# The third batch's k, q and v asked for behind the last weight tile, in a fused pack attention and softplus layer

## The chip, the core and the metric

The kernel runs on one core of a Trainium2 chip. Its engines are TensorE (PE in the rows; its weight loads are PEld), VectorE (DVE), ScalarE (ACT), GpSimd (POOL) and SyncE (SP), which here only issues DMA transfers. The metric is the device time of one execution in microseconds (us), lower is better.

## The reference

Attention goes through a small set of 32 "pack" queries per head: the packs attend to the sequence, and then each query attends to the packs. A two-layer network with softplus follows.

```python
batch, n_heads, seq, head_dim = (8, 8, 576, 64)
n_pack = 32
def sm_attn(qq, kk, vv):
    s = scale * np.matmul(qq, kk.transpose(0, 1, 3, 2))
    s = s - np.max(s, axis=-1, keepdims=True)
    a = np.exp(s)
    a = a / (np.sum(a, axis=-1, keepdims=True) + 1e-09)
    return np.matmul(a, vv)
p_packed = sm_attn(p, k, v)
out = sm_attn(q, p_packed, p_packed)
...
n_tokens, d_model, d_ff = (4608, 512, 2048)
h = x @ w_in
g = np.maximum(h, 0.0) + np.log1p(np.exp(-np.abs(h)))
return (g @ w_out).astype(np.float32)
```

The weights `w_in` and `w_out` come as float64; the other inputs and the output are float32.

## The kernel before

**Units.** The work is a list of units (b, f): batch b of 8, and f one of 16 blocks of 128 hidden columns. In a unit `gemm1` (L511) multiplies the attention output of the batch by a block of the first weights into two PSUM tiles `ph`, `softplus` (L546) turns them into `e` on ScalarE and VectorE and splits `e` into a high and a low part `gh` and `gl`, and `gemm2_tile` (L569), two units later, adds their products with `w_out` into four accumulators `acc`. There are two `ph` buffers, so a unit's first product waits until the softplus step of the unit before has read them (L558). The four accumulators have one buffer each: a batch's first product into `acc` 2 waits until the last batch's `acc` 2 has been copied out to `o` (L588, in `store`).

**The attention of the next batch** is a generator, `attention(b)`; its steps are drawn between the tiles of the units of batch b - 1. For batches 0 and 1 the transposes of k and q are made on TensorE, from batch 2 (`BY_BLOCK`) on by VectorE (L253), from k and q loaded in four parts of 32 rows each (L133). `load` (L114) is called from within the generator, early: the k and v of batch b + 1 are asked for while batch b's attention runs, so those of batch 2 during the units of batch 0. All these loads share four buffers (`ld`); a load waits for the reader of the buffer's last content.

**The first weights are folded.** `make_m` (L482) multiplies the packed values of a batch by `w_in` itself, and the result takes the place of the first weights. For batch 0 it does so for 256 columns at a time, products 0 to 7 (`psm_0_c`); product c is emitted at the end of unit 2c - 2, and its halves `mh` and `ml` serve units 2c and 2c + 1.

**The weights are converted on the chip** during batch 0 by the generator `convert` (L162), 32 tiles in the order i0 i1 o0 o1 i2 i3 o2 o3 and so on (i of `w_in`, o of `w_out`). A tile is loaded as raw 64-bit words into `x_i` or `x_o` (`load64`, L140; from the ninth on two buffers serve), read twice by ScalarE (L188 makes `m`, L192 makes `r`), put together by VectorE (L194, L199) and GpSimd (L207), which writes `w_in_sb` or `t`. The load of tile n + 2 reuses the buffer of tile n. Product 7 of batch 0 needs tiles i14 and i15, numbers 28 and 29 of the order.

**What sets the order.** TensorE's instructions run in the order in which they are written. On the other engines, SyncE's queue among them, the framework's scheduler sets the order when the kernel is built; each engine then runs its queue strictly in that order.

## Time and profile before

| | us |
|---|---|
| median of 3 runs | 789.79 (789.66 to 790.73) |
| the profiled execution | 791.07 |
| its span, first to last instruction | 789.2 |
| TensorE busy | 744.0 (94%) |
| VectorE busy | 532.9 (68%) |
| ScalarE busy | 436.5 (55%) |

The table is read from the top: how long the kernel takes, how long the one execution took that the profile describes, and how much of its span each engine worked. An engine that is busy nearly all the time bounds the kernel over the whole, but single stretches can have another limit.

### The profile page before, as it was taken

Reading aid. Unit: us, or ns where it says so; the run is one execution under the profiler, and the core shown is the slowest. Engines: PE = TensorE matmul, PEld = TensorE weight load, DVE = VectorE, ACT = ScalarE, POOL = GpSimd, SP = SyncE. Lnnn points to the kernel's source line nnn. Section 1 sums busy time; section 2 is a strip of 40 time slices with the busy share of each in tenths; the row PEclk is TensorE's granted clock in tenths of the full one; section 3 lists DMA queues with packets and bytes.
Section 4 is the critical chain, followed back from the end, with each engine's and each line's share of the span. In section 5 each row is a group of like instructions: output and inputs, shape, how many; then the busy total and the mean of one; then the engine's idle time right before and its main releaser. Section 6 shows DMA issues by size and latency. Waiting matters only on the chain.

```text
span 789.2 us, 14442 instructions
## 1 busy us (share of the span) xinstructions
PE 744.0 (94%) x5436; PEld 589.1 (75%) x5436; DVE 532.9 (68%) x1264; ACT 436.5 (55%) x1085; POOL 91.2 (12%) x166
## 2 busy tenths in 40 slices
PE   6879978399999999999999999999999999999997
PEld 4756756287778877887878787877788777878886
DVE  2688758767578665977487665966597656865554
ACT  5678856466556264566556265565555354555540
POOL 1415322210000000000000000000000000000010
PEclk9799989599999999999999999999999999999999
DMA  9976746703421242124411151124312210010002
GB/s 219 245 178 178 165 110 134 153 14 85 68 53 31 68 74 49 31 48 85 74 31 32 66 90 33 32 71 80 56 31 44 67 17 2 1 54 1 1 1 67
DMA packets 163397, 55.97 MB, mean 71 GB/s; under 512 B 143872, under 2 KB 156672, under 8 KB 163328
## 3 DMA queue, kind: packets, MB, share of 16 engines
q1 hardware_dynamic: 162784, 54.93, 32.3%
q8 instruction: 42, 0.69, 0.4%
q14 instruction: 27, 0.22, 0.1%
q10 hardware_dynamic: 544, 0.13, 0.1%
HBM read 45.61 MB, written 9.44 MB: 70 GB/s over the span
## 4 chain that ended last, share of the span: by engine, by line
PE 75%; DVE 1%; ACT 1%; DMA 0%; issue 0%; ACTq 0%; DVEq 0%
PE acc L571 38%; PE ph L527 23%; PE acc_m L571 6%; PE psm L490 3%; PE ps L270 2%; PE psp L325 1%; PE psa L315 1%; DVE at_l L472 1%; ACT e L554 0%; ACT e L553 0%; DMA out<-o 0%; DVE e L558 0%; ACT e L555 0%; ACT at_h L286 0%; PE psx L338 0%
## 5 line engine op out<-in xcount | busy, mean ns | idle before, releaser
L553 ACT ACTIVATE e<-ph 128x288 f32<-128x288 f32 x256 | 103.0, 402 | 213.5 <-PE ph L527 190.8
L558 DVE SCALAR_TENSOR_TENSOR e<-ph,e 128x288 f32<-128x288 f32 x256 | 113.7, 452 | 153.4 <-ACT e L555 153.1
L571 PE MATMUL acc<-wo_h,gh 128*128 128x512 f32 x512 | 208.1, 407 | 0.4 <-DVE o L588 0.4
L571 PE MATMUL acc<-wo_h,gl 128*128 128x512 f32 x512 | 201.1, 393 | 0.0
L571 PE MATMUL acc<-wo_l,gh 128*128 128x512 f32 x512 | 201.1, 393 | 0.0
L527 PE MATMUL ph<-at_h,mh 128*128 128x288 f32 x512 | 159.0, 311 | 3.9 <-DVE e L558 3.1
L527 PE MATMUL ph<-at_l,mh 128*128 128x288 f32 x512 | 153.6, 300 | 2.5 <-DVE at_l L472 2.4
L527 PE MATMUL ph<-at_h,ml 128*128 128x288 f32 x512 | 152.8, 298 | 0.0
L527 PEld LDWEIGHTS ph<-at_h,mh 128*128 128x128 f32 x512 | 97.6, 191 | 40.9 <-issue 13.6
L571 PEld LDWEIGHTS acc<-wo_h,gh 128*128 128x128 f32 x512 | 96.6, 189 | 26.3 <-issue 9.8
L564 POOL COPY rest<-e 128x64 f32<-128x64 f32 x128 | 46.2, 361 | 587.5 <-DVE e L558 581.5
L571 PEld LDWEIGHTS acc<-wo_h,gl 128*128 128x128 f32 x512 | 96.3, 188 | 21.6
L554 ACT ACTIVATE e<-e 128x288 f32<-128x288 f32 (+1 forms) x240 | 109.2, 455 | 3.5
L555 ACT ACTIVATE e<-e 128x288 f32<-128x288 f32 (+1 forms) x240 | 109.4, 456 | 2.9
L571 PEld LDWEIGHTS acc<-wo_l,gh 128*128 128x128 f32 x512 | 96.7, 189 | 13.1
L527 PEld LDWEIGHTS ph<-at_l,mh 128*128 128x128 f32 x512 | 97.9, 191 | 7.2 <-DVE at_l L472 4.5
L527 PEld LDWEIGHTS ph<-at_h,ml 128*128 128x128 f32 x512 | 97.8, 191 | 0.0
L544 DVE TENSOR_TENSOR gl<-e,gh 128x512 fp32r<-128x512 f32 x128 | 87.0, 680 | 5.3
L490 PE MATMUL psm<-w_in_sb,pt 64*32 64x512 f32 (+1 forms) x576 | 39.4, 569 | 23.5 <-POOL w_in_sb L207 20.6
L543 DVE CAST gh<-e 128x512 fp32r<-128x512 f32 x128 | 56.2, 439 | 5.8
L505 ACT CAST mh<-psm 128x512 fp32r<-128x512 f32 (+1 forms) x72 | 35.7, 542 | 43.8 <-PE psm L490 43.6
L506 DVE TENSOR_TENSOR ml<-psm,mh 128x512 fp32r<-128x512 f32 (+1 forms) x72 | 42.8, 622 | 18.6 <-ACT mh L505 18.6
(77 smaller groups left out, 742.8 us busy)
## 6 DMA issues: line engine op xcount, KB each, us to landing
v<-in_v SPq DMA_DIRECT2D x16, 576.0 KB, 5.0
x_i<-in_moe_w_in SPq DMA_DIRECT2D x32, 256.0 KB, 4.8
x_o<-in_moe_w_out SPq DMA_DIRECT2D x16, 512.0 KB, 3.9
k<-in_k SPq DMA_DIRECT2D x48, 144.0 KB, 3.3
q<-in_q SPq DMA_DIRECT2D x48, 144.0 KB, 3.2
out<-o SPq DMA_DIRECT2D x24, 256.0 KB, 2.0
k<-in_k SPq DMA_DIRECT2D x4, 576.0 KB, 9.8
q<-in_q SPq DMA_DIRECT2D x4, 576.0 KB, 8.6
```

The source lines that it names most:

```text
L490: nc.tensor.matmul(ps[hh * J:(hh + 1) * J, :n], res["pt"][g][o:o + D, hh * J:(hh + 1) * J], w_in_sb[o:o + D, hh, c * n:(c + 1) * n], start ...
L505: nc.scalar.copy(mh[:, cols], ps[:, :n])
L506: nc.vector.tensor_tensor(ml[:, cols], ps[:, :n], mh[:, cols].bitcast(F32), op=ALU.subtract)
L527: nc.tensor.matmul(ph[:, :C], x[:, ms], y[:, g, cs], start=(i == 0), stop=(i == 3 * G - 1),)
L543: nc.vector.tensor_copy(hi, x)
L544: nc.vector.tensor_tensor(lo, x, hi.bitcast(F32), op=ALU.subtract)
L553: nc.scalar.activation(es[c], hv[c], AF.Abs)
L554: nc.scalar.activation(e[:, x], e[:, x], AF.Exp, scale=-1.0)
L555: nc.scalar.activation(e[:, x], e[:, x], AF.Ln, bias=1.0)
L558: nc.vector.scalar_tensor_tensor(es[c], hv[c], 0.0, es[c], op0=ALU.max, op1=ALU.add)
L564: nc.gpsimd.tensor_copy(rest[:, rest_at(b, f), r:r + REST], e[:, NT * P:])
L571: nc.tensor.matmul(acc, x[:, cs], y[:, f, :], start=(first and i == 0), stop=(last and i == 2),)
```

## The change

Loads of k, q and v of batch 2 no longer go out when `load` is called. Until the weights are all asked for they are put on a list, `late`; three steps from the end of the conversion's order, where the last tile has just been asked for, `release` issues what is on the list. Those loads, and any of batch 2 that come later, are tied to the last weight load: `tc.issue_after(last_weight.ins)` makes the scheduler place them behind it on SyncE. It adds an order within that queue, and no semaphore. The loads themselves, their sizes and buffers are the same, and nothing is computed differently. Behind the change a line's number is some 9 to 21 higher.

```diff
--- before.py
+++ after.py
@@ -1,5 +1,5 @@
 import math
-from contextlib import ExitStack
+from contextlib import ExitStack, nullcontext
 
 import concourse.bass as bass
 import concourse.tile as tile
@@ -110,10 +110,19 @@
             nc.scalar.copy(dst[D:], ps[:D])
 
     loaded = {}
+    late = []
 
     def load(nm, b, g):
         if b >= B:
             return
+        if late is not None and b == BY_BLOCK:
+            late.append((nm, b, g))
+            return
+        with tc.issue_after(last_weight.ins) if b == BY_BLOCK else nullcontext():
+            load_now(nm, b, g)
+
+    def load_now(nm, b, g):
+
         src = {"q": q, "k": k, "v": v}[nm][b, g * HG:(g + 1) * HG]
         if b < BY_BLOCK:
             t = ld.tile([NP, HG, SI, D], F32, tag="ld", name=f"{nm}_{b}_{g}")
@@ -135,14 +144,24 @@
                 )
         loaded[nm, b, g] = t
 
+    def release():
+
+        nonlocal late
+        late, todo = None, late
+        for x in todo:
+            load(*x)
+
+    last_weight = None
+
     CN = 512
 
     def load64(srcs, nm, tag="x"):
         pool, bufs = (cv, 2) if tag == "x" else (work, 1)
         x = pool.tile([P, CN], I64, tag=tag, name=f"x_{nm}", bufs=bufs)
         n = P // len(srcs)
+        nonlocal last_weight
         for i, src in enumerate(srcs):
-            nc.sync.dma_start(
+            last_weight = nc.sync.dma_start(
                 x[i * n:(i + 1) * n].rearrange("x (a n) -> x a n", a=src.shape[1]), src
             )
         return x
@@ -219,6 +238,8 @@
                 first(n)
                 if n < 6 or n >= 8:
                     prefetch(n + 4 if n < 6 else n + 2)
+                if n + 3 == len(order):
+                    release()
             yield
             w, i = order[n - 1] if n else ("i", 0)
             t = ts.pop(n - 1)[0].bitcast(F32) if n else None
```

Since the scheduler places the instructions of SyncE, ScalarE, VectorE and GpSimd, the change moves more than the loads. Three places follow, first before and then after. A name's numbers are batch, head group and so on; the last one is a buffer number.

SyncE's queue around the last weight tiles, before (`x_i14` is the load of tile 14 of `w_in`):

```order
L133 DMA k_2_1_1397<-in_k 32x36x32 x3
L145 DMA x_o12_1415<-in_moe_w_out 128x512
L145 DMA x_o13_1489<-in_moe_w_out 128x512
L125 DMA v_2_0_1513<-in_v 96x24x64
L145 DMA x_i14_1503<-in_moe_w_in 64x4x128 x2
L145 DMA x_i15_1561<-in_moe_w_in 64x4x128 x2
L145 DMA x_o14_1602<-in_moe_w_out 128x512
L125 DMA v_2_1_1749<-in_v 96x24x64
L145 DMA x_o15_1674<-in_moe_w_out 128x512
L133 DMA q_2_0_2098<-in_q 32x36x32 x4
L98 DMA p_1_4006<-in_p 32x8x64 x4
```

The same place after:

```order
L164 DMA x_o12_1405<-in_moe_w_out 128x512
L164 DMA x_o13_1479<-in_moe_w_out 128x512
L164 DMA x_i14_1493<-in_moe_w_in 64x4x128 x2
L164 DMA x_i15_1549<-in_moe_w_in 64x4x128 x2
L164 DMA x_o14_1590<-in_moe_w_out 128x512
L164 DMA x_o15_1662<-in_moe_w_out 128x512
L142 DMA k_2_0_1664<-in_k 32x36x32 x4
L142 DMA k_2_1_1669<-in_k 32x36x32 x4
L134 DMA v_2_0_1674<-in_v 96x24x64
L134 DMA v_2_1_1749<-in_v 96x24x64
L614 DMA out_0<-o_0_0_2034 96x512
L614 DMA out_0<-o_0_0_2034 32x512
```

The last parts of k, and v, no longer stand between the weight tiles but behind the last of them; q of batch 2 and the second load of p now stand further down, among the stores `out`.

ScalarE around unit 12's softplus, before (`m_26` and `r_26` are the two reads of tile 26 of the order, which is `x_o12`; `e_0_12` is the softplus of unit 12 of batch 0):

```order
L263 COPY T_q_1_1_3_1729<-psT_q_1_1_3_1725 128x288
L555 ACTIVATE e_0_12_1715<-e_0_12_1715 128x576
L188 ACTIVATE m_26_1497<-x_o12_1415 128x512
L192 ACTIVATE r_26_1499<-x_o12_1415 128x512
L192 ACTIVATE r_27_1557<-x_o13_1489 128x512
L188 ACTIVATE m_27_1555<-x_o13_1489 128x512
L226 CAST wo_h_88<-t_26_1501 128x512
L226 CAST wo_h_88<-t_27_1559 128x512
L361 ACTIVATE a2_1_1_0_1756<-a2_1_1_0_1756 128x288
L361 ACTIVATE a2_1_1_1_1763<-a2_1_1_1_1763 128x288
L188 ACTIVATE m_28_1596<-x_i14_1503 128x512
L192 ACTIVATE r_28_1598<-x_i14_1503 128x512
```

After, one unit earlier in the program:

```order
L211 ACTIVATE r_28_1586<-x_i14_1493 128x512
L247 CAST wo_h_88<-t_27_1547 128x512
L526 CAST mh_0_6_0_1610<-psm_0_6_1_1601 128x256
L574 ACTIVATE e_0_11_1630<-ph_0_11_0_1616 128x288
L574 ACTIVATE e_0_11_1630<-ph_0_11_1_1623 128x288
L575 ACTIVATE e_0_11_1630<-e_0_11_1630 128x576
L576 ACTIVATE e_0_11_1630<-e_0_11_1630 128x576
L284 COPY T_q_1_1_1_1644<-psT_q_1_1_1_1640 128x288
L211 ACTIVATE r_29_1658<-x_i15_1549 128x512
L382 ACTIVATE a2_1_0_1_1515<-a2_1_0_1_1515 128x288
L284 COPY T_q_1_1_2_1684<-psT_q_1_1_2_1680 128x288
L207 ACTIVATE m_29_1656<-x_i15_1549 128x512
```

The reads of `x_i14` and `x_i15` (`m_28`, `r_28`, `m_29`, `r_29`) stood behind the end of unit 12's softplus; now they stand around unit 11's.

VectorE at the start of batch 1, where batch 0's output is copied out of the accumulators, before:

```order
L588 COPY o_0_2_2051<-acc_0_2_805 128x512
L558 SCALAR_TENSOR_TENSOR e_1_2_2082<-ph_1_2_0_2068,e_1_2_2082 128x288
L558 SCALAR_TENSOR_TENSOR e_1_2_2082<-ph_1_2_1_2075,e_1_2_2082 128x288
L253 STREAM_TRANSPOSE T_k_2_1_0_2126<-k_2_1_1397 128x288
L588 COPY o_0_3_2062<-acc_0_3_806 128x512
L295 TENSOR_REDUCE m1_2_0_2122<-a1_2_0_1991 128x1
L543 CAST gh_1_2_2128<-e_1_2_2082 128x512
L297 TENSOR_SCALAR nm1_2_0_2124<-m1_2_0_2122 128x1
L253 STREAM_TRANSPOSE T_k_2_1_1_2181<-k_2_1_1397 128x288
L544 TENSOR_TENSOR gl_1_2_2129<-e_1_2_2082,gh_1_2_2128 128x512
L253 STREAM_TRANSPOSE T_k_2_1_2_2193<-k_2_1_1397 128x288
L307 TENSOR_SCALAR rs_2_0_2190<-z1_2_0_2179 128x1
```

After:

```order
L274 STREAM_TRANSPOSE T_k_2_1_0_2126<-k_2_1_1669 128x288
L316 TENSOR_REDUCE m1_2_0_2122<-a1_2_0_1991 128x1
L564 CAST gh_1_2_2128<-e_1_2_2082 128x512
L318 TENSOR_SCALAR nm1_2_0_2124<-m1_2_0_2122 128x1
L274 STREAM_TRANSPOSE T_k_2_1_1_2181<-k_2_1_1669 128x288
L565 TENSOR_TENSOR gl_1_2_2129<-e_1_2_2082,gh_1_2_2128 128x512
L274 STREAM_TRANSPOSE T_k_2_1_2_2193<-k_2_1_1669 128x288
L328 TENSOR_SCALAR rs_2_0_2190<-z1_2_0_2179 128x1
L274 STREAM_TRANSPOSE T_k_2_1_3_2228<-k_2_1_1669 128x288
L329 RECIPROCAL rs_2_0_2190<-rs_2_0_2190 128x1
L609 COPY o_0_2_2051<-acc_0_2_805 128x512
L609 COPY o_0_3_2062<-acc_0_3_806 128x512
```

The copies `o_0_2` and `o_0_3`, which stood ahead of unit 2's softplus step and behind its first k transpose, now stand together behind four k transposes and a reciprocal.

## Rows read from the trace of the kernel before

**Rows 1.** The execution as a whole: span and mean granted TensorE clock.

```profile
core 0: 789.2 us, clock 0.975
```

**Rows 2.** Waits of TensorE in the whole execution: us in total, times, longest.

```profile
PE psm L490 <- POOL w_in_sb L207: 20.6, 3, 15.5
```

**Rows 3.** Stretches: us, busy time by engine (instructions), PEclk, DMA share, GB/s.

```profile
54.50:93.99 39.49, 34.57 (x274) 25.71 (x275) 31.27 (x68) 33.21 (x73) 17.14 (x17) 0.96 0.64 166
93.99:163.26 69.27, 48.37 (x363) 37.48 (x363) 49.23 (x111) 40.92 (x84) 19.43 (x21) 0.83 0.59 129
...
106.25:109.90 3.65, 0.00 (x1) 0.00 (x1) 1.81 (x4) 2.74 (x5) 1.27 (x1) 0.81 0.29 59
109.90:115.26 5.36, 5.36 (x31) 4.27 (x32) 2.40 (x6) 2.61 (x7) 1.27 (x1) 0.50 0.54 159
...
136.27:151.79 15.52, 0.00 (x0) 0.00 (x0) 13.51 (x31) 6.38 (x11) 5.37 (x4) 0.60 0.70 157
151.79:156.30 4.51, 4.51 (x29) 3.61 (x30) 2.37 (x5) 1.76 (x5) 1.27 (x1) 0.50 0.99 189
```

**Rows 4.** Timeline of TensorE: the three products that waited for w_in_sb.

```profile
109.90 1.11 PE L490 MATMUL psm<-w_in_sb,pt 64*32 64x256 f32 x16 [3.65 <-POOL w_in_sb L207]
...
124.98 0.67 PE L490 MATMUL psm<-w_in_sb,pt 64*32 64x256 f32 x16 [1.42 <-POOL w_in_sb L207]
...
151.79 1.11 PE L490 MATMUL psm<-w_in_sb,pt 64*32 64x256 f32 x16 [15.52 <-POOL w_in_sb L207]
```

**Rows 5.** Timeline of SyncE's queue, 117 to 139 us.

```profile
117.09 3.29 SPq L133 DMA_DIRECT2D k<-in_k  x3
120.48 2.45 SPq L145 DMA_DIRECT2D x_o<-in_moe_w_out  x2
122.99 0.42 SPq L125 DMA_DIRECT2D v<-in_v  x1
135.56 3.10 SPq L145 DMA_DIRECT2D x_i<-in_moe_w_in  x4
```

**Rows 6.** Timeline of ScalarE, 134 to 149 us.

```profile
134.30 0.67 ACT L188 ACTIVATE m<-x_o 128x512 f32<-128x512 f32 x1
134.87 1.22 ACT L192 ACTIVATE r<-x_o 128x512 int32<-128x512 uint32 x2
...
148.54 0.65 ACT L192 ACTIVATE r<-x_i 128x512 int32<-128x512 uint32 x1
```

**Rows 7.** DMA issues, 88 to 124 us: count, KB each, median us to landing.

```profile
x_i<-in_moe_w_in SPq DMA_DIRECT2D x8, 256.0 KB, 4.3
x_o<-in_moe_w_out SPq DMA_DIRECT2D x4, 512.0 KB, 3.9
k<-in_k SPq DMA_DIRECT2D x8, 144.0 KB, 4.2
```

**Rows 8.** Timeline of VectorE around the stores of batch 0.

```profile
168.53 0.82 DVE L558 SCALAR_TENSOR_TENSOR e<-ph,e 128x288 f32<-128x288 f32 x2
...
180.47 0.69 DVE L588 COPY o<-acc 128x512 f32<-128x512 f32 x1 [1.42 <-DMA out<-o]
...
182.20 0.65 DVE L588 COPY o<-acc 128x512 f32<-128x512 f32 x1
...
185.21 0.47 DVE L253 STREAM_TRANSPOSE T_k<-k 128x288 f32<-128x288 f32 x1
...
186.77 0.15 DVE L308 RECIPROCAL rs<-rs 128x1 f32<-128x1 f32 x1
```

**Rows 9.** Timeline of TensorE around the same stores.

```profile
169.04 0.40 PE L527 MATMUL ph<-at_h,mh 128*128 128x288 f32 x1
...
181.64 0.40 PE L571 MATMUL acc<-wo_h,gh 128*128 128x512 f32 x1
...
182.91 0.51 PE L571 MATMUL acc<-wo_h,gh 128*128 128x512 f32 x1 [0.41 <-DVE o L588]
```

**Rows 10.** Timeline of ScalarE: the sum of the third batch's first exponential.

```profile
184.69 0.19 ACT L302 ACTIVATION_READ_ACCUMULATOR a<-a,nm 128x1 f32 x1
```

## The prediction

> **What bounds the kernel now.** I read the whole first, then the waits of TensorE, then stretches of time, and then each engine's timeline around the one long wait. The span is 789.2 us at a mean granted clock of 0.975 [rows 1]. TensorE is the bound over the long run, so a wait taken out of it comes off the end, unless another engine fills the hole. The largest wait by far is that of `make_m` for converted columns of `w_in`: 20.6 us in three pieces [rows 2], before products 5, 6 and 7 of batch 0: 3.65, 1.42 and 15.52 us [rows 4]. All three lie in units 7 to 14 of batch 0 (93.99 to 163.26 us), which take 69.27 us while TensorE is busy for 48.37 [rows 3]. The clock adds to it: after the 3.65 and the 15.52 us of idleness TensorE ran 5.36 and 4.51 us at 0.50, the lower of its two levels [rows 3].
>
> Why is tile 15 of `w_in` late? The reader should see that SyncE is not the one that holds it. The queue passes the third batch's k at 117.09 and asks for the `w_out` tiles 12 and 13 from 120.48 on; then it stands still until 135.56 [rows 5]. At that moment ScalarE ends its first read of tile 12: m at 134.30, r from 134.87 (two of 0.61) [rows 6]. There are two staging buffers, so tile 14 of `w_in` can't be asked for before that read. Tiles land in 3.9 to 4.3 us (median) [rows 7], so those asked for from 120.48 lay ready from about 124.5 on, some 10 us before ScalarE came to them. In ScalarE's queue that read stands behind the softplus of unit 12; the order printed above shows it.
>
> **The change, part by part.** Four terms.
>
> (1) *The weights, units 7 to 14.* With the k and v loads out of the way the scheduler sets the reads of the weight tiles earlier: the last `w_in` tile is now read ahead of the softplus of unit 12 and not behind it. So all three waits should go, and with them the slow clock. This is a gain from the order on ScalarE, more than from freed DMA time. Its size lies between bounds. From above: TensorE's own need, 48.37 less at most half of the 9.87 us that it ran at half clock, is 43.4 us, a gain of 25.8. But VectorE is busy for 49.23 us of the same work [rows 3] and can't do it in less; the gain is then 20.0. From below: units 1 to 6, which also convert two tiles a unit and never wait for `w_in`, take 39.49 us, 6.58 each [rows 3]; eight of them are 52.7 us, a gain of 16.6. I take the middle of the last two, 51.3 us, a gain of **18.0**: VectorE has the last softmax and the conversions of all remaining tiles between two softplus steps here, so it becomes the bound, and some of its waits show.
>
> (2) *The third batch's first k on VectorE.* Its four transposes, 0.47 each [rows 8], lay in the 15.52 us hole before, when nobody was delayed. Now the load comes later, and they stand near the end of unit 14, ahead of the low parts of the attention output and of the softplus of unit 15, on which the first product of batch 1 waits: 168.53, with the product at 169.04 [rows 8, 9]. Cover gone: four by 0.47, 1.9 us, less the 0.5 us between that softplus step's start and the product, a loss of about **1.3** (bounds 0, if VectorE has run ahead, and 1.9).
>
> (3) *The copies of the first batch's output.* Before, accumulators 2 and 3 were copied out at 180.47 and 182.20 [rows 8], and TensorE wrote the next accumulators 2 and 3 at 181.64 and 182.91 [rows 9]. Now both copies stand behind four transposes of k and behind a reciprocal that needs the sum of the exponential, which ScalarE gives out at 184.69 plus 0.19 [rows 10]. Counted on the clock of before: that sum is there at 184.9, or some 0.7 earlier, since one copy of 0.65 is out of the way of the maximum that the exponential needs; the transpose behind it and the reciprocal take 0.47 and 0.15 [rows 8]; the copy starts at about 185.1 and ends at 185.8. Accumulator 2 is written from 185.85 in place of 181.64, 4.2 us of a standing TensorE. Accumulator 3 follows 0.7 later, and without its wait of before; at its end the loss is 3.4 us. Nothing hides this: TensorE's queue holds accumulator 2 at its head, and all later work of batch 1 behind it. Loss **3.4**.
>
> (4) *The clock after (3).* The row of 3.65 us of idleness was followed by 5.36 us at 0.50 [rows 3], half of which, at most 2.7, is lost; a standing still of 4.2 us is nearest to that row. I take **2.2**; bounds 0 and 2.7.
>
> Other moves cost nothing that I can find. The second load of p is asked for a batch later, and needed only in batch 3. The third batch's q is asked for around the first stores; its transposes come some units later, behind that batch's second softmax sum, and a load of this kind lands in about 4.2 us [rows 7].
>
> The k, q and v are the same bytes, so nothing else is added. The sum: 18.0 - 1.3 - 3.4 - 2.2 = 11.1 us, a span of 778.1 us. The profiled execution itself took 791.07 us, 1.87 around its span, and lies 1.28 above the median of the three timed runs, 789.79. I take the gain off the median: **778.7 us**.
>
> Is the data now late? At 6.4 us a unit the product 7 falls at about 132.4, and the last tile is asked for about then. Four parts of k at 1.1 us of queue each (three took 3.29 [rows 5]) and 4.2 us to land [rows 7] give 141; the transposes are due near 145.3, the end of unit 14. That leaves some 4 us. The Trainium skill speaks against the change here: its page "DMA: Bandwidth & Descriptors", section "Rules for kernel authors", says to issue a DMA early and to wait for it late, so that its cost lies under compute. By that rule the loads, of which the last k went at 117.09 before and now would go after 132, would show as waits of VectorE, rival D below; the rows leave room for them, so the trace as far as it goes does not bear the rule out here.
>
> **The rivals.**
> A. *TensorE stays the bound.* VectorE's 49.23 us contain the long hole, in which nothing pressed it, so its real need may be smaller. Then (1) gives up to 25.8, and if the clock in (4) also holds, 25.8 - 1.3 - 3.4 = 21.1: 768.7 us. Against it: VectorE was busy for 13.51 of the 15.52 us of that hole [rows 3], so it was not loitering.
> B. *ScalarE stands in front of a tile that has not landed.* The new order puts reads between the parts of the softplus (tile 13 of `w_out` ahead of a logarithm). A tile is asked for when the one two before it has been read, and lands 3.9 to 4.3 us later [rows 7]. If half a landing, 2 us, shows in three of the pairs that are left, 6 us go: 784.7 us. Against it: with two tiles a unit in units 1 to 6 this did not stop the kernel more than the 6.58 us a unit already hold.
> C. *The other side: the wait stays.* If the ring of two buffers holds the tiles back whatever the order, product 7 waits as before and (2) to (4) still cost: 789.8 + 6.9 = 796.7 us. It decides if less than 6.9 of the 25.8 us come back. Against it: the 10 us between landing and read of tile 12 are a matter of order.
> D. *The third batch's k is late* and VectorE stands in front of it with batch 1's weights behind. The change turns slower once this wait is over 11.1 us, that is once the k lands some 15 us later than worked out. If it were 13 us: 791.7 us.
>
> **How the numbers follow.** Chances: my forecast 0.64 (its own range 774.5, with 20.0 in (1) and no clock loss, to 781.2, with 16.6, 1.9 and 2.7), A 0.12, B 0.16, C 0.05, D 0.03. The range leaves out A, C and D: 771 to 785. About 0.2%, 1.6 us, is what a measurement of this kernel can tell from no change. My forecast, A and B are all faster, 0.92; C and most of D are slower, 0.06; a chain of losses that ends within 0.2% has 0.02.
>
> **What would show it.** Right: no wait of `psm` for `w_in_sb` over 2 us; units 7 to 14 in 50 to 53 us; VectorE busy above 0.9 of that stretch; a wait of some 4 us of an accumulator for the copy `o` at the start of batch 1, with a clock of 0.50 behind it. Wrong: a long wait of `psm` for `w_in_sb` still there (C), ScalarE waiting for `x_o` or `x_i` for microseconds (B), VectorE waiting for k (D), or no wait at the copies, by which I would be 5.6 us too high.

## The result, and the profile after

| | before | after |
|---|---|---|
| median of 4 runs, us | 789.72 (789.36 to 790.73) | 779.33 (778.38 to 780.04) |
| ratio after to before | | 0.9866 (95% interval 0.9849 to 0.9883) |
| the profiled execution, us | 791.07 | 778.38 |
| its span, us | 789.2 | 776.6 |

The changed kernel is 10.4 us faster; 11.1 us was forecast, and the time lies 0.6 us above the 778.7 predicted. The mean granted clock is 0.989, and was 0.975 [rows 1].

The stretches of the profile after (us, busy time by engine, granted clock, DMA share, GB/s). The first goes from the start of product 4 of batch 0 to the start of product 0 of batch 1, that is units 7 to 14; the second to product 1 of batch 1:

```profile
92.32:145.41 53.09, 47.55 (x363) 35.61 (x362) 50.95 (x108) 40.66 (x84) 20.96 (x21) 0.97 0.67 152
145.41:169.50 24.09, 20.21 (x129) 15.41 (x128) 18.22 (x43) 12.58 (x32) 1.28 (x5) 0.99 0.16 39
167.65:169.50 1.85, 1.85 (x6) 1.04 (x6) 0.54 (x1) 0.00 (x0) 0.00 (x0) 0.82 0.44 123
169.50:173.48 3.98, 3.98 (x29) 2.31 (x29) 1.29 (x2) 1.58 (x4) 0.00 (x0) 0.65 0.94 186
173.48:190.00 16.52, 16.52 (x148) 13.57 (x147) 9.05 (x22) 9.87 (x28) 0.96 (x3) 1.00 0.26 42
```

Units 7 to 14 take 53.09 us in place of 69.27 [rows 3], and VectorE is busy for 50.95 of them, 96%. Products 5, 6 and 7 in TensorE's timeline (start and duration in us, and in brackets the wait), which answer to [rows 4]:

```profile
104.94 1.19 PE L511 MATMUL psm<-w_in_sb,pt 64*32 64x256 f32 x16
...
117.89 1.29 PE L511 MATMUL psm<-w_in_sb,pt 64*32 64x256 f32 x16 [0.65 <-DVE pt L361]
...
134.68 0.91 PE L511 MATMUL psm<-w_in_sb,pt 64*32 64x256 f32 x16 [0.85 <-DVE a L370]
```

None of the three waits for `w_in_sb` any more; what is left ahead of the last two is 0.65 and 0.85 us for VectorE. SyncE's timeline, to be held against [rows 5]:

```profile
106.97 4.73 SPq L164 DMA_DIRECT2D x_o<-in_moe_w_out  x2
113.14 5.43 SPq L164 DMA_DIRECT2D x_i<-in_moe_w_in  x4
120.41 7.66 SPq L164 DMA_DIRECT2D x_o<-in_moe_w_out  x2
128.12 7.38 SPq L142 DMA_DIRECT2D k<-in_k  x8
```

ScalarE's two reads of tile 12 of `w_out`, against [rows 6]:

```profile
111.88 0.67 ACT L207 ACTIVATE m<-x_o 128x512 f32<-128x512 f32 x1 [0.54 <-ACT r L211]
112.44 0.66 ACT L211 ACTIVATE r<-x_o 128x512 int32<-128x512 uint32 x1
```

Tiles 12 and 13 of `w_out` are asked for at 106.97 and not at 120.48, tile 12 is read from 111.88 and not from 134.30, and the loads of tiles 14 and 15 of `w_in` go out at 113.14 and not at 135.56, again at the moment at which the second read of tile 12 ends. VectorE's timeline up to the stores of batch 0, which answers to [rows 8]:

```profile
147.85 0.47 DVE L274 STREAM_TRANSPOSE T_k<-k 128x288 f32<-128x288 f32 x1
...
150.66 0.82 DVE L579 SCALAR_TENSOR_TENSOR e<-ph,e 128x288 f32<-128x288 f32 x2
...
166.50 0.47 DVE L274 STREAM_TRANSPOSE T_k<-k 128x288 f32<-128x288 f32 x1
166.88 0.12 DVE L329 RECIPROCAL rs<-rs 128x1 f32<-128x1 f32 x1
166.92 1.27 DVE L609 COPY o<-acc 128x512 f32<-128x512 f32 x2
```

TensorE's over the same time, against [rows 9]:

```profile
151.17 0.40 PE L548 MATMUL ph<-at_h,mh 128*128 128x288 f32 x1
...
167.65 0.50 PE L592 MATMUL acc<-wo_h,gh 128*128 128x512 f32 x1 [3.74 <-DVE o L609]
```

The copies of accumulators 2 and 3 stand behind the reciprocal (166.88); accumulator 2 is written at 167.65 after a wait of 3.74 us, and right behind it the clock is at 0.82 and 0.65 for 5.8 us (third and fourth window).

Where the 12.6 us between the two spans come from, by landmarks on TensorE:

| stretch | before | after | gain |
|---|---|---|---|
| start to product 4 of batch 0 | 93.99 | 92.32 | 1.67 |
| units 7 to 14 (product 4 to product 0 of batch 1) | 69.27 | 53.09 | 16.18 |
| product 0 to product 1 of batch 1 | 20.55 | 24.09 | -3.54 |
| from there to the end | 605.4 | 607.1 | -1.7 |

The first line can't be put down to the change: in the executions profiled below, product 4 starts anywhere between 90.1 and 95.6 us, with the program ahead of it the same or nearly so. The comparisons below therefore go by stretches first and by totals second. A stretch is read from the one profiled execution of each kernel, a total from all its runs.

### The profile page after: what moved, and what is told of

It is laid out like the page before. It is cut to its first block, busy times and chain, and to the rows that moved or that the text cites. A ratio compares the mean times of both kernels' runs of the same rounds, so it can differ in the third digit from the quotient of the medians.

```text
span 776.6 us, 14447 instructions
## 1 busy us (share of the span) xinstructions
PE 740.8 (95%) x5436; PEld 584.9 (75%) x5436; DVE 535.9 (69%) x1264; ACT 435.3 (56%) x1085; POOL 92.2 (12%) x166
## 4 chain that ended last, share of the span: by engine, by line
PE 81%; DVE 9%; ACT 4%; DMA 3%; issue 1%; POOL 0%; SPq 0%; ACTq 0%; DVEq 0%; POOLq 0%
PE acc L592 40%; PE ph L548 25%; PE acc_m L592 6%; PE psm L511 4%; PE ps L291 3%; PE psp L346 2%; DMA q<-in_q 1%; PE psa L336 1%; DVE e L579 1%; DVE at_l L493 1%; DVE t L218 1%; ACT e L575 1%; DVE t L213 1%; DMA k<-in_k 1%; ACT e L574 1%
## 5 line engine op out<-in xcount | busy, mean ns | idle before, releaser
L564 DVE CAST gh<-e 128x512 fp32r<-128x512 f32 x128 | 57.8, 452 | 5.5
## 6 DMA issues: line engine op xcount, KB each, us to landing
k<-in_k SPq DMA_DIRECT2D x4, 576.0 KB, 10.4
```

The costliest lines, as they stand in the source:

```text
L564: nc.vector.tensor_copy(hi, x)
```

## Experiments

My theory (T1) was the prediction's: the waits go because ScalarE reads the tiles earlier, VectorE then bounds units 7 to 14, and the copies cost what terms 3 and 4 say. The rivals: what counts is that k is out of the tiles' way (in SyncE's queue or in the DMA engines); VectorE is no bound; the loss at the copies would come back elsewhere. One table for all of them; "units 7 to 14" is the stretch of above, "batch 1" goes from its product 0 to its product 2 (two stretches, for the wait at the copies and the clock behind it), and each total stands beside the kernel before on the same chip. The ratio is an estimate from all runs and need not be the quotient of the two medians.

| kernel | units 7 to 14 | batch 1 | total, median (range) | before there | ratio (95%) |
|---|---|---|---|---|---|
| before | 69.27 | 42.03 | 789.72 | | |
| after | 53.09 | 46.86 | 779.33 | 789.72 | 0.9866 (0.9849 to 0.9883) |
| after, again | 52.89 | 47.62 | 778.98 (777.33 to 782.48) | 792.63 | 0.9838 (0.9799 to 0.9877) |
| reads first | 66.04 | 43.04 | 788.38 (786.25 to 794.84) | 791.85 | 0.9970 (0.9949 to 0.9991) |
| ScalarE's order | 58.01 | 43.02 | 781.92 (779.58 to 785.58) | 790.74 | 0.9893 (0.9867 to 0.9919) |
| copies of bytes | 53.74 | 46.80 | 779.73 (776.88 to 780.51) | 790.56 | 0.9856 (0.9826 to 0.9886) |
| tiny copies | 54.07 | 47.49 | 780.12 (778.74 to 784.05) | 790.56 | 0.9876 (0.9840 to 0.9912) |
| k on GpSimd | 61.98 | 43.23 | 783.93 (783.12 to 786.95) | 792.63 | 0.9901 (0.9872 to 0.9929) |
| no tie | 56.33 | 43.03 | 779.29 (777.35 to 779.77) | 791.85 | 0.9840 (0.9820 to 0.9861) |
| copies o first | 53.44 | 43.48 | 775.74 (775.27 to 775.83) | 791.85 | 0.9799 (0.9780 to 0.9817) |
| without wo_l | 50.13 | 46.85 | 777.65 (776.87 to 779.97) | 792.63 | 0.9819 (0.9793 to 0.9846) |
| wo_l twice | 55.84 | 48.25 | 782.45 (780.39 to 785.31) | 792.63 | 0.9877 (0.9846 to 0.9909) |
| wo_l on GpSimd | 53.97 | 46.84 | 782.62 (778.02 to 788.36) | 791.85 | 0.9892 (0.9858 to 0.9926) |
| gh on ScalarE, copies o first | 52.70 | 45.00 | 775.86 (773.75 to 778.78) | 790.56 | 0.9826 (0.9787 to 0.9865) |

### What ends the wait for the weights

**Reads first.** The kernel before, with one edit in `softplus`:

```diff
-                    nc.scalar.activation(es[c], hv[c], AF.Abs)
+                    n = min(2 * f + 6, 29)
+                    with tc.issue_after(read[n].ins) if b == 0 and 10 <= f <= 12 else nullcontext():
+                        nc.scalar.activation(es[c], hv[c], AF.Abs)
```

(`read[n]` is the second read of tile n.) Expected:

> The kernel before with one thing changed: in units 10 to 12 of batch 0 ScalarE's queue holds the reads of the weight tiles ahead of the softplus of the unit. The loads of the third batch's k and v stay early, between the weight tiles, as before. T1 (the order on ScalarE is what the change gives): the wait of 15.5 us of psm for w_in_sb falls under 2 us, the two waits of 3.7 and 1.4 us may stay, units 7 to 14 take 53 to 58 us in place of 69.3, and the kernel 776 to 781 us. T2 (what counts is that k and v are out of the way of the tiles, in the DMA engines and in SyncE's queue): the long wait stays over 10 us and the kernel takes 787 to 790 us.

Measured: 66.04 us for the stretch, 788.38 us in all. The window of the stretch (columns as above):

```profile
93.24:159.28 66.04, 50.73 (x363) 38.51 (x362) 49.19 (x109) 40.83 (x84) 19.89 (x21) 0.87 0.55 125
```

TensorE's waits in it (us in total, times, longest):

```profile
PE ph L529 <- DVE e L562: 10.2, 4, 7.6
PE psm L492 <- POOL w_in_sb L209: 5.1, 2, 3.7
```

The wait of 15.5 us is gone, as T1 said, but a wait of `ph` for the softplus step, 7.6 us, has come in its place: the softplus of unit 10 now stands behind the reads of tile 12 of `w_out`, which is asked for only at 119.57 (120.48 in the kernel before), so it begins at 126.95, and the products of unit 11 wait for its buffer. My form of T1 falls here. Either this order is a poor one, or the tiles are late for another reason as well.

**ScalarE's order.** The same question with the very order of the changed kernel. A list of 103 names holds ScalarE's instructions of units 5 to 15 in the order that they have there, and each is tied behind the last of those that precede it in the list and are already written:

```diff
+    def act(key, f, *args, **kw):
+        i = place.get(key)
...
+        ahead = [j for j in queued if j < i]
+        with tc.issue_after(queued[max(ahead)]) if ahead else nullcontext():
+            queued[i] = f(*args, **kw).ins
...
-                    nc.scalar.activation(es[c], hv[c], AF.Abs)
+                    act(f"ph_{b}_{f}_{c}", nc.scalar.activation, es[c], hv[c], AF.Abs)
```

But for a few neighbours that are swapped, ScalarE's queue is then that of the changed kernel, and SyncE's that of the kernel before. VectorE's order is left to the scheduler. Expected:

> The kernel before, k and v of the third batch early and between the weight tiles as before (SyncE's queue is that of the kernel before up to the last tile), but with ScalarE's instructions of units 5 to 15 of batch 0 tied into the very order that they have in the changed kernel. The copies o 2 and o 3 stand as before. T1 (the order on ScalarE is enough, as the prediction said): no wait of psm for w_in_sb over 2 us, units 7 to 14 in 53 to 56 us, the kernel 772 to 777 us, below the changed kernel, since the copies are not late. T2 (the tiles are late in SyncE's queue, because k's load waits at its head for a free buffer, whatever ScalarE's order): waits of TensorE for w_in_sb or for e of 5 us and more, units 7 to 14 in 58 to 69 us, the kernel 779 to 790 us, and SyncE's k waits 5 us for the reader of its buffer while a tile's buffer is free.

Measured: 58.01 us. The window:

```profile
94.00:152.01 58.01, 49.53 (x363) 37.28 (x362) 49.02 (x109) 40.38 (x84) 20.78 (x21) 0.91 0.63 144
```

SyncE's timeline:

```profile
105.05 0.31 SPq L157 DMA_DIRECT2D k<-in_k  x1
105.47 0.52 SPq L169 DMA_DIRECT2D x_o<-in_moe_w_out  x1
```

ScalarE's second read of tile 11 of `w_in`:

```profile
101.67 0.66 ACT L80 ACTIVATE r<-x_i 128x512 int32<-128x512 uint32 x1
```

SyncE's waits for k in the stretch:

```profile
SPq L157 <- PE psp L349: 7.7, 1, 7.7
```

The stretch, the total and SyncE's wait lie in the ranges of T2, at their near end; but the waits of TensorE that T2 names, for `w_in_sb` or `e`, are not there. The order on ScalarE, with what the scheduler makes of it on the other engines, gives 69.27 - 58.01 = 11.3 of the 16.2 us. What the other 4.9 us hang on is not shown; the trace offers two things.

The first is k at the head of SyncE's queue. Tile 11 of `w_out` takes the buffer of tile 11 of `w_in`, which is free at 101.67 + 0.66 = 102.3; but k's first part stands ahead of it and waits, for 7.7 us and until 105.05, for the matmul that reads v out of the buffer that k is to fill. The tile is asked for at 105.47, some 3 us later than its own buffer allowed.

The second is VectorE's order. TensorE's waits of over 1 us in the stretch are 2.81, 1.33 and 2.55 us, each for a copy `T_q` by ScalarE, and none is for a tile. Ahead of the first of them ScalarE waited 4.36 us for VectorE's step on tile 11 of `w_in`, and VectorE had stood for 3.44 us at `pp`, which waits for the same matmul `psp` as k does. The three rows, of VectorE, ScalarE and TensorE:

```profile
105.06 0.48 DVE L357 TENSOR_SCALAR pp<-psp,rs 128x64 f32<-128x64 f32 x2 [3.44 <-PE psp L349]
...
106.68 0.66 ACT L80 ACTIVATE m<-x_o 128x512 f32<-128x512 f32 x1 [4.36 <-DVE t L223]
...
109.63 1.08 PE L514 MATMUL psm<-w_in_sb,pt 64*32 64x256 f32 x8 [2.81 <-ACT T_q L80]
```

In the changed kernel VectorE does the steps of two more tiles before it comes to `pp` (103.84). When tile 11 of `w_out` is read at last, at 109.97, ScalarE doesn't wait for it: here the late request is covered by the late step of VectorE. The third wait, too, stands behind a wait of ScalarE for such a step, 2.08 us at 125.08. The scheduler sets VectorE's order and SyncE's; whether the one is so because of k's place in the other no run tells.

**Copies of bytes, tiny copies.** If k in the queue costs, is it its bytes, its slots, or its wait? The changed kernel, with eight transfers at k's old places that wait for no buffer:

```diff
+                rows = k[2].rearrange("h s d -> (h s) d").rearrange("(y z a) d -> z y a d", y=P, a=4)
+                for z in {20: [0], 21: [1, 2, 3], 23: [4], 26: [5, 6, 7]}.get(n, []):
+                    t = w_in_sb[:, z % 2 * 2:z % 2 * 2 + 2, (12 + z // 2) * P:(13 + z // 2) * P]
+                    with tc.issue_after(last_weight.ins):
+                        nc.sync.dma_start(t.rearrange("x g (a d) -> x g a d", d=J), rows[z].rearrange("y (g a) (two d) -> y g (a two) d", g=2, d=J))
```

The tiny ones go from `rows[z, :J, :1, :J]` to `t[:J, :1, :J]`.

> The changed kernel with eight extra transfers of parts of k (131 KB each in pieces of 128 bytes, much as k's own 147 KB) put between the weight tiles in SyncE's queue, at the very places where the third batch's k stood before (one before tile 10 of w_in, three before its tile 11, one before tile 11 of w_out, three before its tile 12). They are written over parts of w_in_sb that are not yet filled, so they wait for no buffer; what they bring is not used. The reads on ScalarE keep their places but for a few swaps. T1 (k's place in the queue cost its issue time and its bytes): units 7 to 14 of batch 0 take 57 to 62 us in place of 53, the kernel 783 to 788 us, and a wait of psm for w_in_sb comes back. T2 (what cost was the wait of k's load for a free buffer at the head of the queue, and the order on ScalarE that came of it): the stretch stays at 53 to 55 us and the kernel at 778.5 to 781 us.

> The kernel of the run before with each of the eight extra transfers cut to 32 pieces of 128 bytes (4 KB): the issue slots in SyncE's queue stay, the bytes are gone; every engine's order is the same. T1a (the bytes, that is the DMA engines' time, cost): 53 to 54.5 us for units 7 to 14, the kernel 778.5 to 780.5 us, well below the run with the full transfers. T1b (the issue slots cost): as long as with the full transfers, within 1 us. T2 (neither): both at 53 to 55 us.

Measured: 53.74 us with the full bytes, 54.07 with the tiny ones. The window of the tiny copies:

```profile
93.48:147.55 54.07, 47.83 (x363) 36.03 (x363) 49.72 (x108) 40.76 (x84) 21.06 (x21) 0.97 0.63 150
```

That of the full ones:

```profile
93.41:147.15 53.74, 48.05 (x363) 36.13 (x362) 50.48 (x108) 40.94 (x84) 21.22 (x21) 0.97 0.68 165
```

SyncE's timeline there:

```profile
90.02 1.62 SPq L196 DMA_DIRECT2D w_in_sb<-in_k  x3
...
106.52 1.62 SPq L196 DMA_DIRECT2D w_in_sb<-in_k  x3
```

Against the two profiles of the changed kernel (53.09 and 52.89 us) the full copies cost 0.7 to 0.9 us of the stretch and the tiny ones 1.0 to 1.2, and no wait for `w_in_sb` comes back. T1 falls: with ScalarE's order as in the changed kernel, the DMA engines' time and the eight slots are not what the change gives back. What T2 says of the wait at the head of the queue is not tested by it, since these copies wait for nothing. One more thing is not the same: three of these copies pass SyncE in 1.6 us, where three parts of k take 3.2 to 3.3 [rows 5].

**k on GpSimd.** The kernel before, with k's loads of batch 2 on another queue, as early as before:

```diff
-                nc.sync.dma_start(
+                (nc.gpsimd if nm == "k" and b == BY_BLOCK else nc.sync).dma_start(
                     t[o * J:(o + 1) * J].rearrange("x h n d -> x (h n) d"), blocks[c, w]
```

> The kernel before, with the third batch's k (eight transfers) issued on GpSimd's queue in place of SyncE's, as early as before. Its bytes cross the DMA engines at the same early time, but they don't stand between the weight tiles in SyncE's queue. Scheduled so, ScalarE's queue comes out nearly as in the changed kernel, and the copies o 2 and o 3 stand nearly as before. T1 (k stood in the way in SyncE's queue: its issue time, and its waits for a free buffer at the head of the queue): no wait of psm for w_in_sb over 2 us, units 7 to 14 in 53 to 56 us, the kernel 773 to 780 us. T2 (the DMA engines' share for k is what held the tiles): units 7 to 14 stay at 62 to 69 us and the kernel at 785 to 791 us. If GpSimd, which waits for a free buffer in place of SyncE, holds back w_in_sb: a wait of psm for w_in_sb of 3 to 5 us.

Measured: 61.98 us. The window:

```profile
92.62:154.60 61.98, 50.43 (x364) 38.34 (x363) 52.01 (x109) 40.96 (x84) 24.07 (x26) 0.89 0.57 133
```

GpSimd's timeline at the first part of the second k:

```profile
102.88 0.82 POOL L133 DMA_DIRECT2D k<-in_k  x1 [3.72 <-PE psp L325]
```

The next tile that it makes, and VectorE ahead of that:

```profile
105.50 1.27 POOL L207 TENSOR_TENSOR w_in_sb<-t,r 128x512 int32<-128x512 int32 x1 [1.80 <-ACT e L554]
...
102.62 0.48 DVE L333 TENSOR_SCALAR pp<-psp,rs 128x64 f32<-128x64 f32 x2 [2.82 <-PE psp L325]
```

The wait of 15.5 us is gone though k crosses as early as before, which again speaks against its bytes. GpSimd now stands 3.72 us in wait for the same reader, and TensorE waits 4.9 us for `w_in_sb`: by its words the third case of the expectation. But the one does not come from the other. GpSimd has k's part out at 102.88 + 0.82 = 103.70 and is then idle for 1.80 us, until VectorE's step of the tile has ended (104.67 + 0.69 = 105.36; the profile names ScalarE, which was done earlier), and that step stands again behind `pp` and its wait for `psp`. It is inconclusive for the rest.

**No tie.** The changed kernel without `issue_after` on the loads; they are still written late:

```diff
-        with tc.issue_after(last_weight.ins) if b == BY_BLOCK else nullcontext():
-            load_now(nm, b, g)
+        load_now(nm, b, g)
```

> The changed kernel without the tie to the last weight load: the loads of k and v of batch 2 are still written late in the program, but the scheduler may put them between the weight tiles again, and does so; the reads of the last w_in tile then lie in and behind the softplus of unit 12. The copies o 2 and o 3 stand in their old places. T1 (order of ScalarE's reads decides): a wait of psm for w_in_sb of 5 to 12 us is back, no long wait for the copies, 780 to 787 us. T2 (writing the loads late is enough): no such wait, and with the copies in their old place 774 to 777 us.

Measured: 56.33 us, and a total as that of the changed kernel. The window:

```profile
94.26:150.59 56.33, 47.97 (x363) 35.84 (x362) 47.81 (x112) 40.74 (x84) 19.39 (x21) 0.94 0.62 143
```

TensorE's waits there and at the copies:

```profile
PE psm L510 <- POOL w_in_sb L225: 5.0, 1, 5.0
...
PE acc L591 <- DVE nm L317: 0.7, 1, 0.7
PE acc L591 <- DVE o L608: 0.5, 1, 0.5
```

T1's wait is back, at its lower end (5.0 us), and of the wait at the copies 1.2 us are left (the 0.7 us put down to `nm` end with the copy `o` just ahead of it). The total lies below T1's range and above T2's. The scheduler put k's parts back between the tiles and left the copies `o` near their old places, ahead of and right behind k's first transpose. What the tie gains in the weights, 3.2 us, it loses at the copies and behind them, 3.8 us: with and without it the kernel is the same.

### The copies and the clock

**Copies o first.** The changed kernel, with the transposes of k's second head group and the first maximum of the third batch behind the last copy:

```diff
+        nonlocal last_copy
-        nc.vector.tensor_copy(o, acc)
+        last_copy = nc.vector.tensor_copy(o, acc)
...
-            nc.vector.transpose(dst, src[:, hh].rearrange("x n d -> x (n d)"))
+            with tc.issue_after(last_copy.ins) if (nm, b, g) == ("k", 2, 1) else nullcontext():
+                nc.vector.transpose(dst, src[:, hh].rearrange("x n d -> x (n d)"))
```

(and the same tie on `reduce_max` of `m1` for batch 2, group 0.) Expected:

> The changed kernel with the copies o 2 and o 3 of batch 0 put back ahead of the k transposes of the third batch and of its first softmax maximum on VectorE; the other queues as in the changed kernel. T1 (terms 3 and 4 of the prediction are a cost of the new order on VectorE): the wait of 3.7 us of acc for o falls under 1 us, the clock behind it holds, and the kernel is 3.4 to 5.6 us faster than the changed one, 773.5 to 776 us. T2 (the time comes back as a later wait, for the third batch's first softmax): 778 to 779.5 us, with a new wait of TensorE behind it in units 2 to 5 of batch 1.

Measured: 775.74 us, 3.2 to 3.6 below the two medians of the changed kernel. The windows (units 7 to 14, and the two of batch 1):

```profile
93.10:146.54 53.44, 47.57 (x363) 35.64 (x363) 50.91 (x108) 40.73 (x84) 20.91 (x21) 0.97 0.66 151
146.54:168.54 22.00, 19.96 (x129) 15.42 (x128) 17.22 (x39) 11.71 (x30) 1.27 (x5) 1.00 0.17 38
168.54:190.02 21.48, 21.48 (x186) 17.02 (x186) 13.42 (x34) 13.63 (x35) 1.46 (x4) 1.00 0.50 88
```

TensorE's waits for the copies:

```profile
PE acc L594 <- DVE o L614: 1.9, 1, 1.9
```

The wait falls from 3.7 to 1.9 us and not under 1, but the clock holds at 1.00 and the two stretches of batch 1 take 43.48 us in place of 46.86, and no wait shows later: T1 by its total. Its median is the lowest of these kernels, at 0.980 of the kernel before. Two things limit it. The copies still stand behind the softplus step of unit 2 and its two parts `gh` and `gl` (they start at 166.21), which in the kernel before accumulator 2's copy did not; that is the wait of 1.9 us. And that the clock holds is not secured by this order: in the last run below, with the same wait of 1.9 us at the same copies, the granted clock is 0.94 in the first of the two stretches, and they take 45.00 us.

### Whether VectorE bounds units 7 to 14

**Without wo_l, wo_l twice.** The changed kernel; the subtraction that makes the low part of a `w_out` tile is left out, or made twice, for the last six tiles:

```diff
-                nc.vector.tensor_tensor(
+                n <= 20 and nc.vector.tensor_tensor(
                     wo_l[:, i, :], t, wo_h[:, i, :].bitcast(F32), op=ALU.subtract
...
-        for i, (x, y) in enumerate(((gh, wo_h), (gh, wo_l), (gl, wo_h))):
+        for i, (x, y) in enumerate(((gh, wo_h), (gh, wo_l if f < 10 else wo_h), (gl, wo_h))):
```

```diff
-                nc.vector.tensor_tensor(
+                for _ in range(2 if n > 20 else 1): nc.vector.tensor_tensor(
```

> The changed kernel without the last six low parts of w_out: their subtraction on VectorE (0.66 us each undisturbed, 0.96 in this stretch) is left out, and the products of those six blocks take the high part in place of the low one, so TensorE's work is the same. T1 (VectorE bounds units 7 to 14): the stretch falls by 3.5 to 6 us, to 47 to 49.5 us, and the kernel to 773 to 776 us. T2 (the order and the chain of softplus and conversion bound it): the stretch stays within 1.5 us of 53, and the kernel at 778 to 780 us.

> The changed kernel with the last six low parts of w_out computed twice: six more subtractions on VectorE in units 7 to 14. T1 (VectorE bounds the stretch): 4 to 6 us longer, 57 to 59 us, and the kernel 782 to 786 us. T2 (VectorE has slack there, its idle 2 us and its drawn-out instructions): the stretch grows by under 2 us and the kernel takes 779 to 781.5 us.

The window of the changed kernel on the same chip:

```profile
92.57:145.46 52.89, 47.66 (x364) 35.73 (x363) 50.90 (x108) 40.81 (x84) 20.99 (x21) 0.97 0.66 153
```

Without `wo_l`:

```profile
95.14:145.27 50.13, 46.74 (x364) 34.58 (x363) 46.67 (x103) 40.76 (x84) 20.11 (x21) 1.00 0.71 162
```

With it twice:

```profile
95.55:151.39 55.84, 46.65 (x364) 35.48 (x363) 54.02 (x110) 40.78 (x84) 20.97 (x21) 0.97 0.62 144
```

VectorE's busy time goes 50.90, 46.67, 54.02; the stretch 52.89, 50.13, 55.84. Six subtractions more: 3.12 us of VectorE (four other steps fall behind the stretch's end) and 2.95 of the stretch, nearly one for one. Six fewer: 4.23 us of VectorE and only 2.76 of the stretch; TensorE is then busy for 46.74 of the 50.13, which leaves little more to gain, though that this is the reason is not shown. T1 holds in its direction, but both sizes lie below its ranges (2.8 and not 3.5 to 6; 2.95 and not 4 to 6) and above those of T2. The totals follow upwards (782.45, in T1's range) and less clearly downwards (777.65, where T1 said 773 to 776): in the profiled execution without `wo_l`, product 4 starts 2.6 us later than in that of the changed kernel.

**wo_l on GpSimd.** The same relief without leaving work out:

```diff
-                nc.vector.tensor_tensor(
+                (nc.gpsimd if n > 20 else nc.vector).tensor_tensor(
```

> The changed kernel with the last six low parts of w_out (wo_l, 0.66 us each) made by GpSimd in place of VectorE. T1 (VectorE is the bound of units 7 to 14, as forecast): that stretch takes 49 to 52 us in place of 53.1, VectorE busy about 47 of it, and the kernel is 1 to 4 us faster than the changed one, 775.5 to 778.5 us. T2 (the order of the queues and the chain of softplus bound it, not VectorE's load): 53 us still, 779 to 780 us. If GpSimd holds VectorE up or makes tiles late: slower than 780 us, with waits of VectorE or TensorE for wo_l or t.

Measured: 53.97 us, by the words of that expectation T2; the total, 782.62 us, is that of its third case, in which GpSimd holds VectorE up. The window:

```profile
95.53:149.50 53.97, 47.49 (x364) 34.45 (x363) 50.87 (x103) 40.83 (x84) 29.17 (x27) 1.00 0.63 150
```

GpSimd's timeline at one subtraction:

```profile
126.50 1.55 POOL L253 TENSOR_TENSOR wo_l<-t,wo_h 128x512 fp32r<-128x512 f32 x1 [0.73 <-ACT wo_h L247]
```

VectorE's timeline at two of its subtractions `gl`:

```profile
126.82 1.78 DVE L565 TENSOR_TENSOR gl<-e,gh 128x512 fp32r<-128x512 f32 x1
...
132.81 0.68 DVE L565 TENSOR_TENSOR gl<-e,gh 128x512 fp32r<-128x512 f32 x1
```

But T1 does not fall by it, since VectorE was not relieved: it is busy for 50.87 us with 103 instructions, where it was for 50.95 with 108. The `gl` that starts at 126.82 ends at 128.60, 0.55 us after GpSimd's subtraction has ended (126.50 + 1.55 = 128.05); the one at 132.81, which began ahead of GpSimd's next instruction (133.04), takes 0.68. The same 0.55 us lie between the two ends at the two other long ones (109.57 and 140.42). VectorE stood still while GpSimd's instruction ran. The Trainium skill states this, on its page "SBUF — State Buffer", section "SBUF: two separate sides": a GpSimd instruction that reads SBUF and a VectorE instruction with two inputs in SBUF take turns at one pair of ports, and the one that comes second stands still until the other has ended. The trace agrees: 0.55 us remain of an instruction that takes 0.68 alone.

**gh on ScalarE.** Copies `o` first, and one of VectorE's steps moved to ScalarE:

```diff
-    def split(hi, lo, x):
-        nc.vector.tensor_copy(hi, x)
+    def split(hi, lo, x, copy=None):
+        (copy or nc.vector.tensor_copy)(hi, x)
...
-        split(*done[b, f], e[:, :NT * P])
+        split(*done[b, f], e[:, :NT * P], nc.scalar.copy if b == 0 and 5 <= f <= 13 else None)
```

> The changed kernel with the copies o 2 and o 3 first, as in the earlier run of it, and with the rounding of gh for units 5 to 13 of batch 0 (0.4 to 0.8 us each on VectorE) done by ScalarE, which is busy for 40.7 of the 53 us. T1 (VectorE bounds units 7 to 14): the stretch falls to 50 to 52 us from 53.4, and the kernel takes 772.5 to 775 us, below the version with the copies first alone (775.7). T2 (ScalarE's queue, now fuller, holds the reads of the tiles or the softplus back): 53.5 us or more, 775.5 to 778 us, with waits of ph for e.

Measured, the window of units 7 to 14:

```profile
90.08:142.78 52.70, 48.36 (x364) 35.81 (x363) 48.75 (x101) 44.05 (x92) 21.03 (x21) 0.97 0.65 155
```

The stretch falls by 0.7 us only, to 52.70, with VectorE 2.2 us less busy than in the version with the copies first, and the total does not differ from that version's. VectorE is rid of eight casts `gh`, 0.84 us each on the mean there, but its subtractions `gl` take 1.29 us on the mean in place of 0.67: what stands still beside GpSimd is now another instruction. For the bound it is inconclusive: two of these four runs lie at 773.75 and 774.22, two at 777.50 and 778.78.

**Not tried.** k out of the way with ScalarE's old order: there the reads would have to be tied behind instructions that are written after them, and the tie works the other way only. So how much k's place alone would give is open. Nor did any run set VectorE's order of the changed kernel beside ScalarE's, with k in its old place.

## Why the prediction was right, point by point

**The bound.** Right as a whole: the wait for `w_in_sb` was on the path, and taken out of it, it came off the end.

**"SyncE is not the one that holds it", and the gain is "from the order on ScalarE, more than from freed DMA time".** Right in weight, incomplete in substance. ScalarE's order is worth 11.3 of 16.2 us, and k's bytes and slots some 1 us. But I read SyncE's queue only where tile 15 was late. Some 15 us earlier k stands at its head in wait for the reader of its buffer, as SyncE's timeline in the kernel before shows:

```profile
104.47 0.31 SPq L133 DMA_DIRECT2D k<-in_k  x1
107.84 0.35 SPq L145 DMA_DIRECT2D x_o<-in_moe_w_out  x1
```

And its waits for k in units 7 to 14:

```profile
SPq L133 <- PE psp L325: 5.2, 1, 5.2
```

In the kernel before that was hidden behind ScalarE's order, since tile 11 of `w_out` waited for its own buffer until 107.84 anyway; with ScalarE's order mended it comes to light, 7.7 us long. The change takes away both. Whether k's wait had to go is not shown: in that run the tile that it held back was not waited for, and TensorE's waits go back to late steps of VectorE. The prediction has no word of VectorE's order in this stretch, and the cause of the last 4.9 us stays open.

**Term 1, a gain of 18.0 (bounds 25.8, 20.0, 16.6).** Measured 16.2, just outside the lower bound; the further 1.67 us ahead of the stretch is no part of it. VectorE is the bound, as forecast: it is busy for 96% of the stretch, and the waits that TensorE has left there, 5.4 us in all, are each for VectorE. What I mis-sized is its need. I took 49.23 us as a floor of the same work, and it is neither. It held the four transposes of k, 0.47 us each, that term 2 itself moves out of the stretch; and pressed together VectorE is busy for 50.95 us without them, because its steps get longer: `gh` takes 0.84 us on the mean in place of 0.60, `wo_l` 0.96 in place of 0.74. In that time it stands still beside GpSimd: the three longest `gh`, 1.50 to 1.51 us, each end 0.28 to 0.29 us after a GpSimd instruction, and those with none beside them take 0.41. The sum has a slip too: the middle of 49.23 and 52.7 is 51.0, a gain of 18.3.

**Term 2, a loss of 1.3.** Measured nothing. The product behind product 0 of batch 1 comes 151.17 - 145.41 = 5.76 us after it, and 5.78 before [rows 9]. VectorE comes to its softplus step at 150.66, right behind the transposes and two of the low parts of the attention output, 0.5 us before that product, as before: just in time. That was my lower bound.

**Term 3, a loss of 3.4.** Measured 3.5 between products 0 and 1, with a wait of 3.74 for accumulator 2 and none for 3, as forecast. The mechanism is that of the prediction, to the reciprocal that the copies stand behind. That VectorE had to wait there for the exponential's sum is not so: it works without a gap from 163.32 on, and the copies are late by their place in its queue alone. By its own rows the term is 3.6 and not 3.4 (185.85 and 0.7 later, against 182.91). Of it, "copies o first" gives back 2.1 and "no tie" 2.6 us; the 1.0 us that stays in "no tie" is for the most part the copies' as well: TensorE waits 1.2 us for them there and waited 0.4 before, since the first now stands behind unit 2's softplus step (167.77 and 168.51, the copy at 168.88) and the second behind the maximum (169.48).

**Term 4, a loss of 2.2.** Measured 1.3 in the stretch behind (22.77 against 21.48 us), and some 0.4 us in the rest. The clock fell as forecast, but the part at half clock was 0.82 and 0.65 on the mean over 1.85 and 3.98 us, less than after the wait that I took as its pattern. In the second profile of the changed kernel the wait of 3.7 us is the same, but the two stretches of batch 1 take 47.62 us, 5.6 above the kernel before, where the first has 4.8; terms 3 and 4 together forecast 5.6. So this size varies between executions.

**k's margin.** Forecast 4 us for the four parts of the first head group. Measured some 12: all eight parts are asked for from 128.12 on in 7.38 us, so four by about 131.8, and land 3.8 us later (the median after), at 135.6; the first transpose is at 147.85. Even the last of the eight lands some 8.5 us ahead of that. The end of unit 14 fell where I put it, but the last tile was asked for 4 us earlier, since the reads run well ahead of product 7. So the rule to issue a DMA early, of the Trainium skill's page "DMA: Bandwidth & Descriptors", section "Rules for kernel authors", weighed in the prediction, is not borne out here: VectorE never waits for k though it is asked for later, and the kernel that asks for it early is the slower one.

The mechanisms of terms 1, 3 and 4 are in the main those forecast. That the sum came so near is in part luck, because the errors cancel: term 1 gave 1.8 less than I took, and terms 2 and 4 cost 1.8 less (term 4 with the 0.4 us in the rest). The slips in terms 1 and 3 cancel as well, but for 0.1. And the 0.2% that the prediction takes for what a measurement can tell is too small for a few runs: 17 runs of the kernel before on one chip lie between 789.76 and 796.07 us.

## What to carry to other kernels

A load that waits for a buffer at the head of SyncE's queue holds the loads behind it, whether they share anything with it or not (here a tile was asked for 3 us later than its own buffer allowed); look for what the queue's head waits for, not only for how long its transfers take. Then look whether anyone waited for what it held back: here that was covered by another engine's order. When an ordering tie lets a scheduler reorder other engines, read what moved there too: here the tie was worth 3.2 us of the weights and cost 3.8 at the copies, and a second tie that put the copies ahead of the transposes was worth another 3. A busy time read beside a second engine on the same ports is no floor and no fixed need, and a part of it may be work that the change itself moves elsewhere.

## What the runs showed of the hardware that was not expected

- Six subtractions moved from VectorE to GpSimd relieved VectorE of nothing: 5 instructions fewer, 50.87 us busy in place of 50.95, and its subtractions `gl` took 1.02 us on the mean in place of 0.67. Eight casts moved from VectorE to ScalarE relieved it of 2.2 us and not of their 6.7, since `gl` rose to 1.29 us.
- In the changed kernel VectorE's cast `gh`, with one input, took 0.41 us alone and 1.50 to 1.51 us three times, each of which ended 0.28 to 0.29 us after a GpSimd instruction that was running.
- Eight transfers of 131 KB in pieces of 128 bytes between the weight tiles changed the stretch by less than 1 us, and no more than the same eight cut to 4 KB.
- The same part of k that SyncE passes in 1.1 us on the mean (three in 3.29 [rows 5]; one by itself in 0.31) and that lands in 4.2 us [rows 7] took GpSimd 0.8 to 1.0 us to issue and landed in 5.3 us (median) from there.
